# Packed attention and two MLPs on one core: other scratches and step numbers for the weight sums, earlier x loads, another order of the last products

## The chip, the cores and the metric

The kernel runs on one core of a Trainium2 chip. The metric is the time of one execution in device microseconds (us), taken as the median of several runs. Five queues matter: TensorE (PE, with its weight loads as PEld), VectorE (DVE), ScalarE (ACT), GpSimd (POOL, hardly used) and SyncE (SP), which here issues the DMA transfers. Each engine works through its own instructions in the order in which they were written; it waits when the next one needs something that is not there yet, and everything behind that instruction waits too.

## The reference

```python
def sm_attn(qq, kk, vv):
    s = scale * np.matmul(qq, kk.transpose(0, 1, 3, 2))
    s = s - np.max(s, axis=-1, keepdims=True)
    a = np.exp(s)
    a = a / (np.sum(a, axis=-1, keepdims=True) + 1e-09)
    return np.matmul(a, vv)
p_packed = sm_attn(p, k, v)              # p: 32 packed queries a head
x = sm_attn(q, p_packed, p_packed)       # 8 batches, 8 heads, 576 positions, 64 wide
x = heads side by side                   # 4608 x 512
h = x @ w_in                             # first MLP, 512 -> 2048 -> 512, ELU
x = np.where(h > 0, h, np.exp(np.minimum(h, 0)) - 1) @ w_out
h = x @ w_in2                            # second MLP, a rational function of h
P = a[0] + a[1]*h + a[2]*h**2 + a[3]*h**3
Q = 1 + |b[0]|*|h| + |b[1]|*h**2
out = (P / (Q + 1e-6)) @ w_out2
```

The weights come in float64 and everything is computed to float32 accuracy: each float32 operand is split in a high and a low part, and a product is three TensorE products (high by high, high by low, low by high).

## The kernel before

**Two stages.** Stage A (to about 785 us) does the attention and the first MLP. It runs 256 steps, 32 for each of the 8 batches: 16 tiles `f` of the hidden width for each half `n` of a batch's positions. A step is six products into `h` (L391), the ELU on ACT and DVE (L400 to L416), and twelve products into four accumulators `acc` (L426). At the end of each half, `a_evac` copies the accumulators to `x` (L450, L452: two by ACT, two by DVE), and the next step's products into `acc` wait for that. `x_prep` then makes seven combinations of the quarters of `x`, splits each in high and low, and stores them to `x2d` in DRAM (14 transfers of 144 KB, L478). Stage B does the second MLP in 48 pairs of `f` tiles. Its first products go by seven products of sums (P1 to P7, a Strassen scheme) that read the stored `x2d` and weight sums stored in `s2d`; `prod` is at L692, its output products `out_mm` at L767.

**What sets the order.** The program is written by lists of calls keyed to a step: `at(q, s, fn, ...)` puts a call in list `ldq` (loads), `peq` (TensorE) or `ewq` (ACT and DVE) of step `s`. The loop at step `s` runs `ldq`, the `h` products of step `s+2`, `peq`, the splitting of `g` for `s+1`, the ELU for `s+2`, then `ewq`, then the `acc` products of `s`, then `a_evac` if a half ends. Each engine's queue gets its instructions in that order.

**Side work in stage A.** During batches 1 to 4 the loop over `i` makes the sums of the second MLP's input weights. In group `i` four pieces `a21, a22, a11, a12` are loaded into `raw` buffers (`w2_raw`, five steps ahead), turned into float32 by `w2_up` (ACT, L520) and `w2_bits` (DVE, L526, L530), added to `s1..s4` (`w2_sum`, DVE, L629), and each result is split: `w2_hi` (ACT, L634) writes the high part to a tile `whi`, `w2_lo` (DVE, L639) leaves the low part in place and issues two stores of 256 KB on SP (L641). All float32 values live in three scratch tiles `ca`, `cb`, `cc`; a scratch or `whi` is written again only when the store that reads it has landed. In batches 5 to 7 the 16 pieces of the output weights ("o") go the same way to `wo2d`. `load_v`, `load_q1` and, in the last batch, `x_load` (768 KB each, L681, for stage B) share the SP queue with them.

**The end of stage B.** `window(s)` writes pair `s`: P products of pair `s+2`, the function of pair `s+1` on ACT and DVE, and six output products o0 to o5 of pair `s`, in the order of the table `PLAN` (a name ending in 1 or 0 is `f` tile 1 or 0; + is pair `s+2`, - pair `s`, none `s+1`). For `s = 45` the output products are moved: o2 behind P5, o3 to o5 behind all. `tail` writes the last pair's output products, tile 1 first, and the copies and stores of the result, all issued on SP. `WARM` gives the numbers of 128x128 products that are run at the start on a unit matrix; the last entry stands just before the first `h` products.

Of the kernel before, what the change touches and what calls it, by code (L numbers as in the profile page):

```python
# [11 lines left out]
F32R = mybir.dt.float32r  # L12
U32 = mybir.dt.uint32
AF = mybir.ActivationFunctionType
ALU = mybir.AluOpType
# [7 lines left out]
def packed_attention_moe_moe2_kernel(  # L23
# [39 lines left out]
    WARM = (14, 2, 1, 2, 5, 2, 11)  # L63
# [568 lines left out]
    def w2_hi(w):  # L632
        t = T.tile([128, 512], F32R, tag="whi", name=f"whi{w}")
        nc.scalar.copy(t, w2t[w])  # L634
        w2t["hi", w] = t
# [127 lines left out]
    def out_mm(p, i, fs=(1, 0)):  # L763
        for f in fs:
            w = wo2[p, f]
            for k, (g, wx) in enumerate(((0, 0), (0, 1), (1, 0))):
                nc.tensor.matmul(  # L767
                    acc[i], lhsT=g_tile(p, f, g)[:, i * 128:(i + 1) * 128], rhs=w[:, wx, :],
                    start=(p % NPR == 0 and f == 1 and k == 0),
                    stop=(p % NPR == NPR - 1 and f == 0 and k == 2))  # L770
# [3 lines left out]
    def out_ev(p, i, eng, cut=(slice(0, DM),)):  # L774
        o = m2["o"][n_o[0] % 5]
        n_o[0] += 1
        u, end = p // NPR * TU + i % 3 * 128, p // NPR * TU + i % 3 * 128 + 128
        segs = []
        while u < end:
            e = min(end, (u // TR + 1) * TR)  # L780
            segs.append((u, e))
            u = e
        for x in cut:
            (nc.scalar.copy if eng is nc.scalar else nc.vector.tensor_copy)(o[:, x], acc[i][:, x])
            for a, e in segs:
                t0, r = a // TR * TA + i // 3 * TR + a % TR, a - (end - 128)
                nc.sync.dma_start(out=out[t0:t0 + e - a, x], in_=o[r:r + e - a, x])
            eng = nc.vector if eng is nc.scalar else nc.scalar
# [32 lines left out]
    def window(s):  # L821
# [6 lines left out]
        if s == NPAIR - 3:  # L828
            late = [x for x in plan if x[0] in ("o3", "o4", "o5")]
            o2 = plan.index(("o2", s))  # L830
            plan.insert(plan.index(("P5", s + 2)) + 1, ("o2", s))
            del plan[o2]
            plan = [x for x in plan if x not in late] + late
# [6 lines left out]
    def tail():  # L840
        p = NPAIR - 1
        for i in range(6):
            out_mm(p, i, (1,))
        for i in range(6):
            out_mm(p, i, (0,))
            h = DM // 2
            out_ev(p, i, (nc.scalar, nc.vector)[i % 2],
                   (slice(0, h), slice(h, DM)) if i == 5 else (slice(0, DM),))

    with tc.manual_schedule():  # L850
# [193 lines left out]
        for b in range(B - 1):  # L1044
# [18 lines left out]
            if b + 2 < B:  # L1063
                at(ldq, o + (28 if b else 36), load_v, b + 2)
                at(ldq, o + (20 if b else 26), load_k, b + 2)
                at(ldq, o + NS + 10, load_q1, b + 2)
# [8 lines left out]
        def w2_split(s, u, w, dst):  # L1075
            at(ewq, u, w2_hi, w)
            at(ewq, s, w2_lo, w, dst)

        for i in range(4):
# [3 lines left out]
            s1, s2, s3, s4 = (("s", i, j) for j in range(1, 5))  # L1083

# [4 lines left out]
            w2_load(s + 10, a22, "cb")  # L1089
            at(ewq, s + 12, w2_sum, s1, "cc", a21, a22, ALU.add)  # L1090
            w2_split(s + 13, s + 12, a22, dst(P4))
            w2_load(s + 16, a11, "cb")
# [5 lines left out]
            w2_load(s + 32, a12, "cb")  # L1098
            at(ewq, s + 33, w2_sum, s4, "cc", a12, s2, ALU.subtract)
            w2_split(s + 35, s + 34, s2, dst(P6))  # L1100
            w2_split(s + 37, s + 36, a12, dst(P2))
            w2_split(s + 42, s + 41, s4, dst(P3))
        slots = [(5, 11, 12, 13), (5, 16, 18, 19), (5, 23, 25, 29), (5, 31, 32, 33), (6, 6, 7, 8), (6, 10, 11, 12),
                 (6, 13, 14, 16), (6, 23, 25, 29), (6, 31, 32, 33)] + [(7, t, t + 1, t + 2) for t in range(3, 22, 3)]
        for i, (b, s, u, t) in enumerate(slots):
            f = i // 2 + NPR * (i % 2)
            w2_load(b * NS + s, ("o", f), ("ca", "cb", "cc")[i % 3])
            w2_split(b * NS + t, b * NS + u, ("o", f), o2_dst(f))
# [29 lines left out]
        for j in range(5):  # L1138
            at(ldq, o + 2 + 2 * j, x_load, 0, j)
# [114 lines left out]
```

## Time and profile before

| | us |
|---|---|
| median of 3 runs | 1532.81 (1527.85 to 1533.84) |
| the profiled execution | 1534.12 |
| its span, first to last instruction | 1532.2 |
| PE busy | 1477.8 (96%) |
| DVE busy | 1245.3 (81%) |
| ACT busy | 1088.0 (71%) |

The busy shares are means over unlike stages. In stage B a pair takes 15.64 us and TensorE hardly pauses; in stage A it pauses in a few places. What a change is worth is read at those places: which engine waits there, for what, and how much of that TensorE feels.

### The profile page before, as it was taken

The page shows a single profiled execution, that of the slowest core. Times are in us where ns is not written, and L with a number is a line of the kernel's source. Part 1 is how long each engine was busy: PE and PEld are TensorE (multiplying, and loading weights), DVE is VectorE, ACT ScalarE, POOL GpSimd, SP SyncE. Part 2 cuts the span into 40 slices and gives each one's busy share as a digit, 9 for nine tenths or more (in the row PEclk, how much of TensorE's full clock was granted, in tenths as well). Part 3 has the DMA queues.
Part 4 walks back from the last instruction along what each step waited for, and adds up shares of the span by engine and source line. Part 5 has one row for each costly group of instructions (what it writes and reads, how often), then busy time and mean ns, then how long its engine had stood idle before and what let it go on. Part 6 is the DMA issues. An engine that isn't in the chain of part 4 may idle for free.

```text
span 1532.2 us, 26764 instructions
## 1 busy us (share of the span) xinstructions
PE 1477.8 (96%) x10194; PEld 1332.4 (87%) x10194; DVE 1245.3 (81%) x2078; ACT 1088.0 (71%) x1992; POOL 3.3 (0%) x8
## 2 busy tenths in 40 slices
PE   7899999989899899999999999999999999999997
PEld 6778979879798798989989888988899888988896
DVE  6887676866768567776589999999999999999996
ACT  4876666666667567776688787778778777778775
POOL 0000000000000000000000000000000000000000
PEclk8999999999999999999999999999999999999999
DMA  9532554354553454538868866777777686777641
GB/s 346 177 140 70 162 181 137 118 156 144 162 153 115 123 171 153 151 106 281 269 218 278 292 226 223 246 246 240 247 240 250 219 280 211 251 258 229 199 147 46
DMA packets 191264, 301.14 MB, mean 197 GB/s; under 512 B 13472, under 2 KB 131488, under 8 KB 190240
## 3 DMA queue, kind: packets, MB, share of 16 engines
q1 hardware_dynamic: 191136, 299.42, 60.0%
q8 instruction: 81, 1.33, 0.4%
q14 instruction: 47, 0.39, 0.1%
HBM read 233.84 MB, written 65.54 MB: 195 GB/s over the span
## 4 chain that ended last, share of the span: by engine, by line
PE 76%; DMA 8%; DVE 8%; ACT 5%; issue 1%; SPq 1%; ACTq 0%; DVEq 0%
PE bank L692 22%; PE acc L426 18%; PE acc L767 17%; PE h L391 8%; PE acc_h L767 8%; DMA x2d<-x 2%; PE m L347 1%; DVE g L406 1%; DVE gl_all L416 1%; ACT g L401 1%; DVE w L744 1%; PE pp L248 1%; ACT g L400 1%; DMA raw0('o', 0)_112<-in_w_out_dram 1%; ACT gl_all L411 1%
## 5 line engine op out<-in xcount | busy, mean ns | idle before, releaser
L426 PE MATMUL acc<-gl_all,wo 128*128 128x288 f32 x3072 | 462.5, 299 | 31.4 <-ACT x L450 17.6
L426 PEld LDWEIGHTS acc<-gl_all,wo 128*128 128x128 f32 x3072 | 419.0, 190 | 79.6 <-ACT g L401 20.2
L391 PE MATMUL h<-A_flat,m 128*128 128x288 f32 x1536 | 245.6, 295 | 2.2 <-DVE m L361 0.9
L391 PEld LDWEIGHTS h<-A_flat,m 128*128 128x128 f32 x1536 | 217.6, 190 | 4.0 <-DVE m L361 1.7
L767 PE MATMUL acc<-wo,A_flat 128*128 128x512 f32 x768 | 204.2, 393 | 0.0
L692 PE MATMUL bank<-xs_wi,sw 128*128 128x384 f32 x960 | 190.1, 336 | 0.3 <-DVE h L710 0.3
L416 DVE TENSOR_TENSOR gl_all<-g,gl_all 128x288 fp32r<-128x288 f32 x256 | 115.7, 452 | 87.6 <-ACT gl_all L411 87.1
L692 PE MATMUL bank<-xs,sw 128*128 128x384 f32 x912 | 180.0, 336 | 3.7 <-DVE h L710 3.1
L692 PEld LDWEIGHTS bank<-xs_wi,sw 128*128 128x128 f32 x960 | 170.4, 188 | 9.8 <-DVE h L710 0.7
L744 DVE SCALAR_TENSOR_TENSOR w<-w,sq 128x768 f32<-128x768 f32 x192 | 178.8, 952 | 0.0
L406 DVE SCALAR_TENSOR_TENSOR g<-g,h 128x288 f32<-128x288 f32 x256 | 115.8, 452 | 73.2 <-ACT g L401 71.0
L692 PEld LDWEIGHTS bank<-xs,sw 128*128 128x128 f32 x912 | 161.7, 188 | 13.6 <-DVE h L710 4.1
L411 ACT CAST gl_all<-g 128x288 fp32r<-128x288 f32 x256 | 110.7, 433 | 87.4 <-PE acc L426 50.8
L767 PEld LDWEIGHTS acc<-wo,A_flat 128*128 128x128 f32 x768 | 142.5, 188 | 21.4
L400 ACT ACTIVATE g<-h 128x288 f32<-128x288 f32 x256 | 105.1, 410 | 52.0 <-PE h L391 51.5
L401 ACT ACTIVATE g<-g 128x288 f32<-128x288 f32 x256 | 113.9, 445 | 8.1
L767 PE MATMUL acc_h<-wo,A_flat 128*128 128x512 f32 x384 | 104.3, 393 | 0.0
L726 DVE SCALAR_TENSOR_TENSOR w<-sq,cf,w 128x768 f32<-128x768 f32 x96 | 97.5, 1015 | 2.1 <-ACT w L716 0.4
L748 DVE SCALAR_TENSOR_TENSOR t<-t,cf,w 128x768 f32<-128x768 f32 x96 | 97.5, 1016 | 1.7
L740 ACT ACTIVATE sq<-sq,cf 128x768 f32<-128x768 f32 x96 | 89.8, 935 | 1.6
L737 ACT ACTIVATE sq<-w,cf 128x768 f32<-128x768 f32 x96 | 89.8, 935 | 1.1 <-DVE w L726 1.1
L758 ACT CAST A_flat<-t 128x768 fp32r<-128x768 f32 x72 | 60.3, 837 | 36.3 <-DVE t L748 36.3
(419 smaller groups left out, 1957.2 us busy)
## 6 DMA issues: line engine op xcount, KB each, us to landing
sw<-s2d SPq DMA_DIRECT2D x144, 512.0 KB, 4.2
wo<-wo2d SPq DMA_DIRECT2D x96, 512.0 KB, 5.0
x2d<-x SPq DMA_DIRECT2D x210, 144.0 KB, 2.4
xs_wi<-x2d SPq DMA_DIRECT2D x20, 768.0 KB, 7.4
xs<-x2d SPq DMA_DIRECT2D x19, 768.0 KB, 7.4
sw<-s2d SPq DMA_DIRECT2D x48, 256.0 KB, 2.8
q<-in_qT_dram SPq DMA_DIRECT2D x16, 576.0 KB, 5.6
v<-in_v_dram SPq DMA_DIRECT2D x8, 1024.0 KB, 6.5
```

The lines of the kernel that those rows point to most:

```text
L391: nc.tensor.matmul(ps[:, :TA], lhsT=m[:, wx, r, c0:c0 + 128], rhs=A[:, ax, r, :], start=(i == 0), stop=(i == 5))
L400: nc.scalar.activation(d["e"], d["h"][:, :TA], AF.Exp)
L401: nc.scalar.activation(d["e"], d["e"], AF.Relu, scale=-1.0, bias=1.0)
L406: nc.vector.scalar_tensor_tensor(d["g"], d["e"], -1.0, d["h"][:, :TA], ALU.mult, ALU.max)
L411: nc.scalar.copy(d["ghi"], d["g"])
L416: nc.vector.tensor_tensor(d["glo"], d["g"], d["ghi"].bitcast(F32), ALU.subtract)
L426: nc.tensor.matmul(acc[m][:, :TA], lhsT=w[:, wx, m * 128:(m + 1) * 128], rhs=d[g], start=(first and i == 0), stop=(last and i == 2))
L692: nc.tensor.matmul(m2["ab"][bank][:, :TU], lhsT=w[:, j % 2, wx, k, :], rhs=x[:, xx, k, :], start=(start and i == 0), stop=(i == 5), skip_g ...
L726: nc.vector.scalar_tensor_tensor(w, m2["sq", f], cf[:, 5:6], w, ALU.mult, ALU.add)
L744: nc.vector.scalar_tensor_tensor(w, w, c, m2["sq", f], ALU.add, ALU.mult)
L748: nc.vector.scalar_tensor_tensor(t, t, cf[:, 0:1], m2["w", f], ALU.add, ALU.mult)
L767: nc.tensor.matmul(acc[i], lhsT=g_tile(p, f, g)[:, i * 128:(i + 1) * 128], rhs=w[:, wx, :], start=(p % NPR == 0 and f == 1 and k == 0), st ...
```

## The change

It does six things. (1) In the weight sums, scratches `cb` and `cc` take turns: piece a22, a11 and sum s4 go to `ta`, sum s1 and piece a12 to `tb`, and `ta`, `tb` are `cb`, `cc` in even groups and `cc`, `cb` in odd ones. Sum s1 and the split of a22 come a step sooner, the split of s4 too. (2) `load_v` is two steps later in batches 1 to 5. (3) In the last batch the high parts of the o pieces take turns in `whi`, `E` and `aT`. (4) The first five `x_load` calls move from steps 226, 228, 230, 232, 234 to 223, 224, 225, 226, 227. (5) The last `WARM` entry is 8, not 11. (6) At the end, pair 45's o2 to o5 stand among P7, P4 and P3; the window of pair 46 follows a table `LAST` that ends tile 1's function before most of tile 0's; `tail` runs the products with the high part of `g` of several accumulators before those with the low part, and the stores of what ACT copied are issued from ACT's queue.

```diff
-    WARM = (14, 2, 1, 2, 5, 2, 11)
+    LAST = (
+        "C12 Id1 Q1 o0 Ln1 ta1 tb1 o1 Exp1 o2 Sq0 Abs0 Na1 Id0 o3 Nb1 Q0 o4 Ln0 g1 o5 hi1 ta0 Exp0 lo1 tb0 Na0 Nb0 "
+        "g0 hi0 lo0").split()
+    WARM = (14, 2, 1, 2, 5, 2, 8)
...
-    def w2_hi(w):
-        t = T.tile([128, 512], F32R, tag="whi", name=f"whi{w}")
+    def w2_hi(w, tag="whi"):
+        t = T.tile([128, 512], F32R, tag=tag, name=f"whi{w}", bufs=tag_bufs.get(tag, 1))
...
-    def out_mm(p, i, fs=(1, 0)):
+    def out_mm(p, i, fs=(1, 0), ks=(0, 1, 2)):
         for f in fs:
             w = wo2[p, f]
-            for k, (g, wx) in enumerate(((0, 0), (0, 1), (1, 0))):
+            for k in ks:
+                g, wx = ((0, 0), (0, 1), (1, 0))[k]
...
-                nc.sync.dma_start(out=out[t0:t0 + e - a, x], in_=o[r:r + e - a, x])
+                (q and eng is nc.scalar and q or nc.sync).dma_start(
+                    out=out[t0:t0 + e - a, x], in_=o[r:r + e - a, x])
...
         if s == NPAIR - 3:
-            late = [x for x in plan if x[0] in ("o3", "o4", "o5")]
-            o2 = plan.index(("o2", s))
-            plan.insert(plan.index(("P5", s + 2)) + 1, ("o2", s))
-            del plan[o2]
-            plan = [x for x in plan if x not in late] + late
+            for x, y in (("o2", "P7"), ("o3", "P4"), ("o4", "P3"), ("o5", "o4")):
+                plan.remove((x, s))
+                plan.insert(plan.index((y, s + 2 * (y[0] == "P"))) + 1, (x, s))
+        elif s == NPAIR - 2:
+            plan = [(x, s + (x[0] != "o")) for x in LAST]
...
         p = NPAIR - 1
+        for k in (0, 1), (2,):
+            for i in range(6):
+                out_mm(p, i, (1,), k)
+        for k in (0, 1), (2,):
+            for i in range(3):
+                out_mm(p, i, (0,), k)
         for i in range(6):
-            out_mm(p, i, (1,))
-        for i in range(6):
-            out_mm(p, i, (0,))
+            if i > 2:
+                out_mm(p, i, (0,))
...
-                at(ldq, o + (28 if b else 36), load_v, b + 2)
+                at(ldq, o + (30 if b else 36), load_v, b + 2)
...
+            ta, tb = ("cc", "cb") if i % 2 else ("cb", "cc")
...
-            w2_load(s + 10, a22, "cb")
-            at(ewq, s + 12, w2_sum, s1, "cc", a21, a22, ALU.add)
-            w2_split(s + 13, s + 12, a22, dst(P4))
-            w2_load(s + 16, a11, "cb")
+            w2_load(s + 10, a22, ta)
+            at(ewq, s + 11, w2_sum, s1, tb, a21, a22, ALU.add)
+            w2_split(s + 12, s + 11, a22, dst(P4))
+            w2_load(s + 16, a11, ta)
...
-            w2_load(s + 32, a12, "cb")
-            at(ewq, s + 33, w2_sum, s4, "cc", a12, s2, ALU.subtract)
+            w2_load(s + 32, a12, tb)
+            at(ewq, s + 33, w2_sum, s4, ta, a12, s2, ALU.subtract)
...
-            w2_split(s + 42, s + 41, s4, dst(P3))
+            w2_split(s + 41, s + 40, s4, dst(P3))
...
-            w2_split(b * NS + t, b * NS + u, ("o", f), o2_dst(f))
+            w2_split(b * NS + t, b * NS + u, ("o", f), o2_dst(f), ("whi", "E", "aT")[i % 3] if b == B - 1 else "whi")
...
         for j in range(5):
-            at(ldq, o + 2 + 2 * j, x_load, 0, j)
+            at(ldq, o - 1 + j, x_load, 0, j)
```

SP's queue around steps 59 to 66 (the first group; `v` is `load_v`, `s2d` takes a weight sum's two parts, `raw1` is a weight piece), before:

```order
L502 DMA raw1('i', 0, 2)_2637<-in_w_in_dram 128x1024
L478 DMA x2d<-x_47_2259 128x2x144 x4
L128 DMA v_2674<-in_v_dram 128x4x512
L131 DMA v_2674<-in_v_dram 64x512
L641 DMA s2d<-whi('i', 0, 0)_2654 128x4x128
L641 DMA s2d<-w2('i', 0, 0)_cb 128x4x128
L502 DMA raw1('i', 2, 1)_2886<-in_w_in_dram 128x1024
```

and in the change, where the scratch names in the queue show nothing yet, but the two stores stand ahead of `v`:

```order
L505 DMA raw1('i', 0, 2)_2634<-in_w_in_dram 128x1024
L481 DMA x2d<-x_47_2256 128x2x144 x4
L644 DMA s2d<-whi('i', 0, 0)_2651 128x4x128
L644 DMA s2d<-w2('i', 0, 0)_cb 128x4x128
L131 DMA v_2738<-in_v_dram 128x4x512
L134 DMA v_2738<-in_v_dram 64x512
L505 DMA raw1('i', 2, 1)_2883<-in_w_in_dram 128x1024
```

Moved: the stores of piece a11 and `load_v` have changed places; nothing else has at this place.

SP's queue in the last batch, from the load of piece o12 on (`xs_wi` is `x_load`, `wo2d` takes an o piece's two parts, `x2d` the x combinations), before:

```order
L502 DMA raw1('o', 12)_8461<-in_w_out_dram 128x1024
L502 DMA raw1('o', 5)_8564<-in_w_out_dram 128x1024
L641 DMA wo2d<-whi('o', 4)_8547 128x512
L641 DMA wo2d<-w2('o', 4)_cc 128x512
L681 DMA xs_wi<-x2d 128x4x384
L478 DMA x2d<-x_223_8529 128x2x144 x2
L502 DMA raw1('o', 13)_8654<-in_w_out_dram 128x1024
L681 DMA xs_wi<-x2d 128x4x384
L641 DMA wo2d<-whi('o', 12)_8670 128x512
L641 DMA wo2d<-w2('o', 12)_ca 128x512
L478 DMA x2d<-x_223_8529 128x2x144 x4
L681 DMA xs_wi<-x2d 128x4x384
```

and in the change:

```order
L505 DMA raw1('o', 12)_8458<-in_w_out_dram 128x1024
L684 DMA xs_wi<-x2d 128x4x384 x2
L505 DMA raw1('o', 5)_8564<-in_w_out_dram 128x1024
L684 DMA xs_wi<-x2d 128x4x384
L644 DMA wo2d<-whi('o', 4)_8547 128x512
L644 DMA wo2d<-w2('o', 4)_cc 128x512
L684 DMA xs_wi<-x2d 128x4x384
L481 DMA x2d<-x_223_8528 128x2x144 x2
L684 DMA xs_wi<-x2d 128x4x384
L505 DMA raw1('o', 13)_8655<-in_w_out_dram 128x1024
L644 DMA wo2d<-whi('o', 12)_8670 128x512
L644 DMA wo2d<-w2('o', 12)_ca 128x512
```

Moved: four of the x loads now stand ahead of the first `x2d` stores of `x_223`, where one stood.

DVE's queue for the last pair, from the first `ta` that moves (L726 and L729 are `Q`, L730 and L733 `ta`, L734 and L737 `tb`, L744 and L747 `Na` and `Nb`, L748 and L751 `g`, L761 and L764 `lo`; before, `w_9293` and `t_9295` are tile 1 and `w_9296` and `t_9298` tile 0), before:

```order
L730 TENSOR_TENSOR t_9298<-t_9298,h_9666 128x768
L734 SCALAR_TENSOR_TENSOR t_9295<-t_9295,cf,h_9301 128x768
L726 SCALAR_TENSOR_TENSOR w_9296<-sq_9297,cf,w_9296 128x768
L744 SCALAR_TENSOR_TENSOR w_9293<-w_9293,sq_9294 128x768
L734 SCALAR_TENSOR_TENSOR t_9298<-t_9298,cf,h_9666 128x768
L744 SCALAR_TENSOR_TENSOR w_9293<-w_9293,sq_9294 128x768
L744 SCALAR_TENSOR_TENSOR w_9296<-w_9296,sq_9297 128x768
L748 SCALAR_TENSOR_TENSOR t_9295<-t_9295,cf,w_9293 128x768
L744 SCALAR_TENSOR_TENSOR w_9296<-w_9296,sq_9297 128x768
L748 SCALAR_TENSOR_TENSOR t_9298<-t_9298,cf,w_9296 128x768
L761 TENSOR_TENSOR g_9665<-t_9295,A_flat 128x768
L761 TENSOR_TENSOR g_9302<-t_9298,xg_k 128x768
```

and in the change, where `w_9290` and `t_9292` are tile 1, `w_9293` and `t_9295` tile 0:

```order
L733 TENSOR_TENSOR t_9292<-t_9292,h_9298 128x768
L737 SCALAR_TENSOR_TENSOR t_9292<-t_9292,cf,h_9298 128x768
L747 SCALAR_TENSOR_TENSOR w_9290<-w_9290,sq_9291 128x768 x2
L729 SCALAR_TENSOR_TENSOR w_9293<-sq_9294,cf,w_9293 128x768
L751 SCALAR_TENSOR_TENSOR t_9292<-t_9292,cf,w_9290 128x768
L733 TENSOR_TENSOR t_9295<-t_9295,h_9663 128x768
L764 TENSOR_TENSOR g_9662<-t_9292,A_flat 128x768
L737 SCALAR_TENSOR_TENSOR t_9295<-t_9295,cf,h_9663 128x768
L747 SCALAR_TENSOR_TENSOR w_9293<-w_9293,sq_9294 128x768 x2
L751 SCALAR_TENSOR_TENSOR t_9295<-t_9295,cf,w_9293 128x768
L764 TENSOR_TENSOR g_9299<-t_9295,xg_k 128x768
```

Moved: tile 1's `lo`, which was next to last, now has only one `Q` and one `ta` of tile 0 ahead of it.

## Rows read from the trace of the kernel before

**Rows 1.** The page's first part: busy time, share, instructions of each engine.

```profile
PE 1477.8 (96%) x10194; PEld 1332.4 (87%) x10194; DVE 1245.3 (81%) x2078; ACT 1088.0 (71%) x1992; POOL 3.3 (0%) x8
```

**Rows 2.** Waits: engine, line, waited for; us in total, times, longest.

```profile
PE acc L426 <- ACT x L450: 17.6, 4, 5.0
...
ACT w2('i', 1, 3)_cb L520 <- DMA s2d<-w2('i', 1, 1)_cb: 5.4, 1, 5.4
...
ACT whi('o', 6)_8956 L634 <- DMA wo2d<-whi('o', 13)_8870: 4.7, 1, 4.7
...
ACT whi('i', 2, 3)_3299 L634 <- DMA s2d<-whi('s', 0, 4)_3198: 3.9, 1, 3.9
```

**Rows 3.** SP's timeline at 221 us: start, duration, what was issued.

```profile
221.30 0.37 SPq L128 DMA_DIRECT2D v<-in_v_dram  x1
```

**Rows 4.** The chain that ended last, same place: start, duration, what.

```profile
222.97 6.58 DMA s2d<-w2('i', 0, 0)_cb
```

**Rows 5.** PE's timeline: first and fourth such place, a step with `s1h`, undisturbed steps.

```profile
224.44 1.72 PE L426 MATMUL acc<-gl_all,wo 128*128 128x288 f32 x12
...
235.18 1.01 PE L426 MATMUL acc<-gl_all,wo 128*128 128x288 f32 x5
...
505.59 1.72 PE L426 MATMUL acc<-gl_all,wo 128*128 128x288 f32 x12
...
513.11 3.25 PE L426 MATMUL acc<-gl_all,wo 128*128 128x288 f32 x12 [5.02 <-ACT x L450]
...
518.81 0.40 PE L426 MATMUL acc<-gl_all,wo 128*128 128x288 f32 x1
...
328.55 0.72 PE L182 MATMUL s1h<-k,p 64*32 64x288 f32 x16
...
687.18 1.72 PE L426 MATMUL acc<-gl_all,wo 128*128 128x288 f32 x12
...
691.91 1.72 PE L426 MATMUL acc<-gl_all,wo 128*128 128x288 f32 x12
```

**Rows 6.** Busy time by stretch (PE, PEld, DVE, ACT, POOL), granted clock, DMA share, GB/s.

```profile
515.50:517.00 1.50, 1.50 (x8) 1.50 (x8) 1.47 (x4) 0.43 (x1) 0.00 (x0) 0.50 0.31 98
```

**Rows 7.** PE's timeline at 271 us, where ACT's wait for `whi` of a22 ends.

```profile
271.06 0.40 PE L426 MATMUL acc<-gl_all,wo 128*128 128x288 f32 x1 [0.52 <-ACT gl_all L411]
```

**Rows 8.** PE's timeline in the last batch, steps 235, 239 and 244.

```profile
715.31 1.72 PE L426 MATMUL acc<-gl_all,wo 128*128 128x288 f32 x12
...
727.70 2.19 PE L426 MATMUL acc<-gl_all,wo 128*128 128x288 f32 x12 [2.37 <-ACT gl_all L411]
...
740.96 1.74 PE L426 MATMUL acc<-gl_all,wo 128*128 128x288 f32 x12
```

**Rows 9.** DMA issues of 684 to 712 us: count, KB each, us to landing.

```profile
xs_wi<-x2d SPq DMA_DIRECT2D x4, 768.0 KB, 5.9
...
wo2d<-whi('o', 5)_8766 SPq DMA_DIRECT2D x1, 256.0 KB, 8.2
```

**Rows 10.** SP's timeline in the last batch: the first x load.

```profile
694.54 0.39 SPq L681 DMA_DIRECT2D xs_wi<-x2d  x1
```

**Rows 11.** PE's timeline at the start: the last `WARM` products.

```profile
23.20 4.60 PE L914 MATMUL warm<-ident 128*128 128x128 f32 x22
```

**Rows 12.** DVE's timeline at the start.

```profile
24.05 0.76 DVE L338 TENSOR_TENSOR A_flat<-s2y,A_flat 128x576 fp32r<-128x576 f32 x1 [0.16 <-ACT A_flat L333]
...
29.54 0.45 DVE L406 SCALAR_TENSOR_TENSOR g<-g,h 128x288 f32<-128x288 f32 x1 [1.02 <-ACT g L401]
```

**Rows 13.** PE's timeline at the end: P3, pair 46's output products, pair 47's.

```profile
1503.42 1.31 PE L692 MATMUL bank<-xs,sw 128*128 128x384 f32 x6 [1.69 <-DVE h L710]
...
1511.41 5.60 PE L767 MATMUL acc<-wo,A_flat 128*128 128x512 f32 x24
...
1517.94 0.50 PE L767 MATMUL acc_h<-wo,g 128*128 128x512 f32 x1 [0.48 <-DVE g L761]
```

**Rows 14.** SP's timeline at the end: the last two stores.

```profile
1527.47 1.22 SPq L787 DMA_DIRECT2D out_dram<-h_o  x2
```

More of the change, by code (lines that the diff above doesn't have):

```diff
@@ L772, in packed_attention_moe_moe2_kernel, with out_ev @@
     n_o = [0]
-    def out_ev(p, i, eng, cut=(slice(0, DM),)):
+    def out_ev(p, i, eng, cut=(slice(0, DM),), q=None):
         o = m2["o"][n_o[0] % 5]
@@ L841, in tail @@
         p = NPAIR - 1
+        for k in (0, 1), (2,):
[4 more added lines that the diff above has]
+                out_mm(p, i, (0,), k)
         for i in range(6):
-            out_mm(p, i, (1,))
-        for i in range(6):
-            out_mm(p, i, (0,))
+            if i > 2:
+                out_mm(p, i, (0,))
             h = DM // 2
             out_ev(p, i, (nc.scalar, nc.vector)[i % 2],
-                   (slice(0, h), slice(h, DM)) if i == 5 else (slice(0, DM),))
+                   (slice(0, h), slice(h, DM)) if i == 5 else (slice(0, DM),),
+                   nc.scalar)
     with tc.manual_schedule():
@@ L1073, in w2_load, with w2_split @@
             at(ewq, s, w2_bits, piece)
-        def w2_split(s, u, w, dst):
-            at(ewq, u, w2_hi, w)
+        def w2_split(s, u, w, dst, tag="whi"):
+            at(ewq, u, w2_hi, w, tag)
             at(ewq, s, w2_lo, w, dst)
```

## The prediction

> **What bounds the kernel now.** I read the page's busy shares first: TensorE is busy for 96% of the span [rows 1], so nothing short of its own pauses is worth much, and the question is where these are. The list of waits answers it: one entry, the `acc` products waiting for ACT's copies of the accumulators (L450), holds 17.6 us in four waits [rows 2]. The same list says what ACT waits for just before: `w2_up` of piece a12 into `cb`, held by the landing of the store of `cb`'s old content (a11). There are four such rows, one for each group, of 4.0, 4.8, 5.0 and 5.4 us; the longest is shown [rows 2]. SP's timeline and the chain show why that store is late: the 1 MB load of `v` is issued 1.67 us ahead of it and the store lands 6.58 us after issue [rows 3, 4]. So the order is: `v` load, store, `w2_up`, `a_evac`, `acc`. Shorter ACT waits of the same sort stand for `whi`, in the groups (3.9 us) and in the last batch (4.7 us) [rows 2].
>
> **Part (1) and (2), the four long waits.** I take the price from TensorE's clock time, not from its idle time, since it restarts slowly. Two undisturbed steps take 691.91 - 687.18 = 4.73 us, and `s1h`, which stands in this stretch, about 0.64 (0.72 less the 0.08 by which neighbours overlap): 5.37 [rows 5]. The first place took 235.18 - 224.44 = 10.74, the fourth 518.81 - 505.59 = 13.22 [rows 5]: 5.4 and 7.85 lost, the least and the most by ACT's waits, mean 6.6, so 26.4 for four. That is more than 17.6 because the clock granted right after such a pause was 0.50, 1.2 GHz instead of 2.4 [rows 6]. In the change a12 goes to `tb`, whose last store (of s1) was issued six steps before, some 14 us, and the a11 store goes ahead of `v`. `w2_up` then has nothing to wait for, and ACT reaches the copies before the accumulators are done. What takes the store's place: s4 now overwrites a11's scratch, four steps (9.4 us) after a11's store, on DVE; with `v` behind it, the store should be down by then. `v` itself is used 11 steps later. At 687 to 692, where a half ends with nothing late, TensorE loses nothing [rows 5]. I take 26, bounds 20 (one of four places finds another late transfer) and 27.
>
> **Part (1), the two-step reuse.** ACT's 3.9 us wait for `whi` (four rows, 3.5 to 3.9) is the s4 store standing behind the load of `q`. TensorE felt 0.52 of it [rows 2, 7]. In the change s4's split comes a step sooner, ahead of `q`, and DVE's sum s1 stands two steps behind that store as before; were it to wait, the low parts of `g` queued behind it on DVE, and so `acc`, would wait too. Four places of 0.5 or a little more: 1.8, bounds 0 (s1 waits again) and 2.7. `q` and the a11 load behind it come a good microsecond later; their users stand about four steps on, so I cost that at nothing; if the cover is gone, ACT waits, and up to 2 us of that is free, as the next part shows.
>
> **Parts (3) and (4), the last batch.** From step 235 at 715.31 to step 244 at 740.96 there are nine steps in 25.65 us [rows 8]; nine undisturbed ones take 9 x 2.365 = 21.3 by rows 5. So 4.4 are lost, nearly all in two `whi` waits and their wake; the longer, 4.7 us on ACT, left TensorE idle for 2.37 [rows 2, 8], so some 2.3 us of an ACT wait cost nothing. With three tiles in turn, a high part is overwritten nine steps after the last, over 20 us: those waits go, +4.4. Against it stands the x loads' move. Before, the first one is issued at 694.54, right ahead of the first x stores of that half [rows 10]; in the change four are ahead of these stores, the first two some ten microseconds before them. A transfer of 256 KB behind two x loads took 8.2 us to land, an x load itself 5.9 [rows 9], so each x load that is still in the queue adds about 3. One more than before will be: the x stores land up to 3 us later, twice an ACT step of `x_prep` waits for them, and 3 - 2.3 = 0.7 is felt each time: -1.4. Later, in exchange, the queue is emptier. Sum +3.0, bounds +4.4 and -4 (four ACT steps that each wait a whole x load, 5.9 - 2.3 = 3.6, less the gain).
>
> Here a rule of the Trainium skill speaks against the change. The rows show transfers landing in the order of issue, the store after the x loads ahead of it [rows 9]. "DMA: Bandwidth & Descriptors", section "Queues, rings and completion order", says that on each DMA engine descriptors are consumed in ring order, though completion is not first in, first out. Taken strictly, the x stores pay for every x load moved ahead of them, and this part would give the lower bound, -4, and a total near 1506; if they passed the loads, it would give +4.4 and a total near 1498. The rows lie between, as the early loads have had time to drain.
>
> **Part (5), the start.** The last `WARM` row is 22 passes in 4.60 us, 0.209 each; three products are six passes, 1.25 us [rows 11]. What they cover: the last input of the first `h` is ready at 24.05 + 0.76 = 24.8, while the row runs to 27.8 [rows 11, 12]. So `h` starts 1.25 earlier. The next consumer is DVE, which idled 1.02 before it [rows 12]; the rest is its own queue. I take 0.8, bounds 0 and 1.25.
>
> **Part (6), the end.** P3 starts 1.69 us late, held by DVE [rows 13]. DVE's order up to there is unchanged, so P3 stays where it is; the gain is that o3 now runs in front of it. Six of the 24 products that take 5.60 us are 1.4 us [rows 13]. Then pair 47's low part of tile 1 no longer comes last but one in the function: by DVE's queue four operations of some 0.95 us fewer stand ahead of it, so the 0.48 pause and its restart, 0.7 together, go [rows 13]. Tile 0's parts come some 0.8 us later than before, but TensorE needs them only after tile 1's 18 products. The last two stores take 1.22 us of SP's queue, one behind the other [rows 14]; on two queues the last is issued up to 0.6 sooner, but ACT's copies now stand behind ACT's issues, which may cost as much: +0.1. No ACT issue is in the trace; its nearest row is SP's 0.61 each. Sum 2.2, bounds 1 and 3.
>
> **Sum.** 26 + 1.8 + 3.0 + 0.8 + 2.2 = 33.8. The profiled execution took 1534.12 with a span of 1532.2; 1534.1 - 33.8 = 1500.3. The median of the runs is 1.3 lower than that execution, so the forecast is 1499.
>
> **Rivals.** (a) The queue gives it back: x loads, `q` and `v` moved in front of or behind other transfers make new ACT waits in the last batch and in the groups. Price: part (4) at -4 instead of +3, the short waits at 0, one long place kept: 7 + 2 + 6 = 15, so 1503 to 1514. For it speaks that an ACT wait stops `a_hi` and `a_evac` alike; against it that 2.3 us of each are free. (b) The long waits stay, because what held ACT was not the scratch but the piece's own load, or the sum's wait moves to DVE: only parts (4) to (6) and half of the rest would come, some 12 us: 1515 to 1526. Against it: the list of waits names the store, and with it the same scratch, in all four. (c) Slower than before: without its pauses TensorE is granted less clock. Place: the rest of the program, stage B above all; price: each microsecond of its work done at 1.2 GHz costs one more, so from 34 us of such work on the gain is gone, 1533 and more. Against it: the clock in the rows fell after pauses, not after work [rows 6], and stage B runs without pauses now.
>
> **How the numbers follow.** The forecast has 0.80, (a) 0.14, (b) 0.04, (c) 0.02. A range of 1493 to 1508 holds the forecast with its bounds (all lows of the parts do not meet; about 9 above, 6 below with the run-to-run spread of before, 1527.85 to 1533.84) and the half of (a) below 1508. Half a per cent, 7.7 us, is about what a measurement of this kernel can tell from no change. All of the forecast and of (a), and (b) below 1525, are faster: 0.97. The same: 0.02. Slower: 0.01.
>
> **What would show it.** In the profile after: no wait of `acc` for L450 over 1 us, and no ACT wait of `w2_up` for an `s2d` store; the stretch that now runs from 505.59 to 518.81 shorter by over 6 us; ACT waiting for x stores in the last batch no more than about 3 us each; TensorE's last pause before P3 shorter by 1.4, and none for tile 1's low part. I am wrong if `acc` waits for L450 again behind another transfer, if waits for `x2d` stores in the last batch add up to more than 10 us, or if the granted clock falls in stage B.

## The result, and the profile after

The changed kernel takes 1496.18 us (median of 4 runs, 1495.55 to 1496.71), the kernel before 1532.87 in the same session: ratio 0.9767, 95% interval 0.9745 to 0.9788. The forecast was 1499 with a range of 1493 to 1508. Below, "after" is the changed kernel; its line numbers are higher than those of before: by 3 in stage A, by 3 to 5 in stage B, by 11 for the warm passes (L914 is L925).

The page's busy times of after, against [rows 1]: the same work in a span of 1493.8 instead of 1532.2.

```profile
PE 1465.7 (98%) x10188; PEld 1325.1 (89%) x10188; DVE 1246.8 (83%) x2078; ACT 1087.0 (73%) x1992; POOL 3.3 (0%) x8
```

The list of waits of after (engine, line, waited for; us in total, times, longest), against [rows 2]:

```profile
ACT x L476 <- DMA x2d<-x: 18.2, 10, 2.9
...
PE acc L429 <- ACT gl_all L414: 2.6, 4, 1.1
...
DVE h_o L788 <- DMA out_dram<-h_o: 2.3, 1, 2.3
...
ACT whi('o', 3)_7946 L637 <- DMA wo2d<-whi('o', 10)_7848: 1.6, 1, 1.6
...
PE acc L429 <- ACT x L453: 0.4, 1, 0.4
```

Of the 17.6 us in which `acc` waited for ACT's copies, 0.4 is left. The `whi` waits of 3.9 and 4.7 are gone. ACT still waits for x stores: over the whole span 18.2 in ten waits, where it was 15.1, none longer than 2.9.

TensorE's timeline of after at the first and the fourth long place (start, duration, what), against [rows 5]:

```profile
222.86 1.72 PE L429 MATMUL acc<-gl_all,wo 128*128 128x288 f32 x12
...
228.27 1.83 PE L429 MATMUL acc<-gl_all,wo 128*128 128x288 f32 x12
...
482.02 1.72 PE L429 MATMUL acc<-gl_all,wo 128*128 128x288 f32 x12
...
487.44 1.83 PE L429 MATMUL acc<-gl_all,wo 128*128 128x288 f32 x12
```

These take 5.41 and 5.42 us, where they took 10.74 and 13.22; the working from undisturbed steps had given 5.37.

TensorE's timeline of after at the end, against [rows 13]:

```profile
1467.35 1.31 PE L695 MATMUL bank<-xs,sw 128*128 128x384 f32 x6 [1.14 <-DVE h L713]
...
1473.98 5.60 PE L771 MATMUL acc<-wo,A_flat 128*128 128x512 f32 x24
1479.42 1.07 PE L771 MATMUL acc_h<-wo,A_flat 128*128 128x512 f32 x4
```

From P3 to the 24 products is 6.63 us, where it was 7.99: 1.36 less. The pause for tile 1's low part, 0.48, is gone. The pause before P3 is 0.55 shorter (1.14 for 1.69), since o2 now stands behind P7 and takes the place of another pause of before, in front of P4:

```profile
1500.42 1.32 PE L692 MATMUL bank<-xs,sw 128*128 128x384 f32 x6 [0.57 <-ACT s L707]
```

P3 starts 8.25 behind P6, where it was 8.26: it stays in its place, and the gain is that o3 now runs ahead of it.

**One table for all kernels.** Rows that each trace has cut the span into five stretches that add up to it: to the second row of `s1h`; on to the last row of `m` products (the groups, where the four long places lie); on to the first P product of stage B (the last batch); on to the end of the last product (stage B); and the rest (the last stores). The last column is the median time of all executions; the five stretches are those of the profiled one. The last batch of after, for one, is 716.82 - 651.41 = 65.41.

| kernel | start | groups | last batch | stage B | stores | time |
|---|---|---|---|---|---|---|
| before | 61.33 | 622.38 | 69.15 | 773.13 | 6.21 | 1532.87 |
| after | 59.73 | 591.68 | 65.41 | 770.92 | 6.06 | 1496.18 |
| after_again | 59.90 | 592.13 | 64.53 | 770.95 | 6.29 | 1495.06 |
| e_scratch | 60.23 | 595.58 | 68.90 | 773.74 | 5.45 | 1505.37 |
| e_v | 59.83 | 595.29 | 70.62 | 773.11 | 5.45 | 1505.56 |
| e_steps | 59.59 | 615.93 | 68.92 | 773.14 | 6.32 | 1526.90 |
| u_xload | 59.76 | 592.50 | 64.64 | 770.96 | 6.74 | 1496.52 |
| u_whi | 59.98 | 592.04 | 64.73 | 770.94 | 6.01 | 1496.21 |
| u_both | 60.37 | 591.80 | 69.53 | 770.99 | 6.11 | 1500.60 |
| u_warm | 60.25 | 590.76 | 64.35 | 770.96 | 6.28 | 1494.37 |
| u_tail | 59.94 | 591.70 | 64.26 | 773.07 | 6.13 | 1497.71 |
| best | 60.32 | 592.07 | 68.20 | 770.97 | 6.74 | 1498.50 |
| lo_first | 60.51 | 592.32 | 64.24 | 770.99 | 6.24 | 1496.95 |
| lo_first_22 | 60.51 | 590.72 | 65.85 | 770.93 | 6.29 | 1495.63 |

Between the first two rows the groups gave 30.7, the last batch 3.7, the start 1.6, stage B 2.2, the stores 0.15: 38.4 of span.

### The profile page after: what moved, and what is told of

It is laid out like the page before. It is cut to its first block, busy times and chain, and to the rows that moved or that the text cites. A ratio compares the mean times of both kernels' runs of the same rounds, so it can differ in the third digit from the quotient of the medians.

```text
span 1493.8 us, 26767 instructions
## 1 busy us (share of the span) xinstructions
PE 1465.7 (98%) x10188; PEld 1325.1 (89%) x10188; DVE 1246.8 (83%) x2078; ACT 1087.0 (73%) x1992; POOL 3.3 (0%) x8
## 4 chain that ended last, share of the span: by engine, by line
PE 87%; DVE 6%; ACT 4%; DMA 2%; issue 1%; ACTq 0%; POOL 0%; DVEq 0%; POOLq 0%
PE acc L429 23%; PE bank L695 23%; PE acc L771 17%; PE h L394 11%; PE acc_h L771 9%; PE m L350 2%; DMA x2d<-xpart 1%; PE pp L251 1%; DVE g L409 1%; DMA x2d<-x 1%; PE s L285 1%; DMA s2d<-w2('i', 2, 2)_cb 1%; DVE gl_all L419 0%; DVE w L747 0%; PE warm L925 0%
## 5 line engine op out<-in xcount | busy, mean ns | idle before, releaser
L429 PE MATMUL acc<-gl_all,wo 128*128 128x288 f32 x3072 | 455.9, 297 | 8.3 <-DVE gl_all L419 2.9
L747 DVE SCALAR_TENSOR_TENSOR w<-w,sq 128x768 f32<-128x768 f32 x192 | 178.9, 952 | 0.1
L419 DVE TENSOR_TENSOR gl_all<-g,gl_all 128x288 fp32r<-128x288 f32 x256 | 115.8, 452 | 60.4 <-ACT gl_all L414 59.7
L751 DVE SCALAR_TENSOR_TENSOR t<-t,cf,w 128x768 f32<-128x768 f32 x96 | 97.5, 1016 | 1.7
L729 DVE SCALAR_TENSOR_TENSOR w<-sq,cf,w 128x768 f32<-128x768 f32 x96 | 97.4, 1015 | 1.6
L761 ACT CAST A_flat<-t 128x768 fp32r<-128x768 f32 x72 | 60.3, 838 | 35.0 <-DVE t L751 35.0
```

Source lines behind the costliest of these rows:

```text
L419: nc.vector.tensor_tensor(d["glo"], d["g"], d["ghi"].bitcast(F32), ALU.subtract)
L429: nc.tensor.matmul(acc[m][:, :TA], lhsT=w[:, wx, m * 128:(m + 1) * 128], rhs=d[g], start=(first and i == 0), stop=(last and i == 2))
L729: nc.vector.scalar_tensor_tensor(w, m2["sq", f], cf[:, 5:6], w, ALU.mult, ALU.add)
L747: nc.vector.scalar_tensor_tensor(w, w, c, m2["sq", f], ALU.add, ALU.mult)
L751: nc.vector.scalar_tensor_tensor(t, t, cf[:, 0:1], m2["w", f], ALU.add, ALU.mult)
```

## The experiments

**Which half removes the long waits?** The change does two things about them, and the prediction credited both together. Each was tried alone on the kernel before. e_scratch:

```diff
+            ta, tb = ("cc", "cb") if i % 2 else ("cb", "cc")
-            w2_load(s + 32, a12, "cb")
-            at(ewq, s + 33, w2_sum, s4, "cc", a12, s2, ALU.subtract)
+            w2_load(s + 32, a12, tb)
+            at(ewq, s + 33, w2_sum, s4, ta, a12, s2, ALU.subtract)
```

(cut: a22 and a11 go to `ta`, s1 to `tb`; no step is moved)

> The kernel before with the turn of the two scratch tiles alone (a12 goes to the tile of s1, s4 to the tile of a11); the load of v stays ahead of the a11 store, and every step stays. Theory A (the wait sits in the choice of scratch): w2_up of a12 finds its tile free, the store of a11, 6.6 us under way, is down before DVE writes s4 over it 9.4 us later; all four long places go, -26, about 1507, no wait of acc for L450. Theory B (it sits in the queue): the store behind v is still late, and now DVE waits for it with the s4 sum; part of the 17.6 us of waits comes back under DVE's name, -10 or less, 1523 or more.

e_v:

```diff
-                at(ldq, o + (28 if b else 36), load_v, b + 2)
+                at(ldq, o + (30 if b else 36), load_v, b + 2)
```

> The kernel before with the load of v two steps later alone, behind the a11 store; scratches and steps as before. Theory A (scratch): w2_up of a12 comes two steps (4.7 us) after the store's issue and is still close behind it; some waits of 1 to 2 us stay, acc feels part: -15 to -20, 1513 to 1518. Theory B (queue): without the 1 MB ahead of it the store lands in some 2 to 3 us like others of its size, before w2_up comes; all four long places go with this one number, -24 to -26, 1507 to 1509. That both the turn and the place of v do it alone would mean that the gains of the two do not add.

Measured: 1505.37 (ratio 0.9817, 0.9803 to 0.9832) and 1505.56 (0.9819, 0.9805 to 0.9834). Either one does the whole of it, and e_scratch's second theory, that DVE would wait in ACT's place, falls; the four places give 26.3 us in both traces. They do not add. Why, the store of a11's low part tells. SP's timeline of e_scratch (start, duration, what):

```profile
220.12 0.37 SPq L128 DMA_DIRECT2D v<-in_v_dram  x1
...
221.78 0.44 SPq L641 DMA_DIRECT2D s2d<-w2('i', 0, 0)_cb  x1
```

and of e_v:

```profile
219.65 0.36 SPq L641 DMA_DIRECT2D s2d<-w2('i', 0, 0)_cb  x1
220.23 0.75 SPq L128 DMA_DIRECT2D v<-in_v_dram  x1
```

The same store in the list of DMA issues (KB each, us to landing), of e_scratch:

```profile
s2d<-w2('i', 0, 0)_cb SPq DMA_DIRECT2D x1, 256.0 KB, 6.3
```

and of e_v:

```profile
s2d<-w2('i', 0, 0)_cb SPq DMA_DIRECT2D x1, 256.0 KB, 2.4
```

In e_scratch the store is as late as in before (6.3 behind `v`; [rows 4] has 6.58), but nobody needs its tile. In e_v the tile is needed as soon as before, but the store lands in 2.4, at 222.05, and `w2_up` comes at 223.66. e_v's first theory, that waits of 1 to 2 us would stay, falls.

**The two-step reuse.** e_steps:

```diff
-            at(ewq, s + 12, w2_sum, s1, "cc", a21, a22, ALU.add)
-            w2_split(s + 13, s + 12, a22, dst(P4))
+            at(ewq, s + 11, w2_sum, s1, "cc", a21, a22, ALU.add)
+            w2_split(s + 12, s + 11, a22, dst(P4))
...
-            w2_split(s + 42, s + 41, s4, dst(P3))
+            w2_split(s + 41, s + 40, s4, dst(P3))
```

> The kernel before with the sum s1, the split of a22 and the split of s4 one step sooner, nothing else. The prediction gave these places 1.8 in all (0 to 2.7); between the two traces TensorE gained 4.4 there. If the step alone does it, -4.4, about 1528.5, with gains of 0.8 to 1.6 at each of the four places and the ACT waits for whi gone. If the prediction's size was right and the rest came from the scratches, -2 or less, 1531 or more.

Measured: 1526.90, ratio 0.9957 (0.9942 to 0.9972), 6.1 us less; at the four places alone 1.59, 1.11, 1.34 and 1.34, together 5.4. The size in the prediction was wrong. Rows of before that it had not used show the rest. From the list of waits:

```profile
DVE w2('s', 1, 1)_cc L629 <- DMA s2d<-w2('s', 0, 4)_cc: 4.2, 1, 4.2
DVE w2('s', 2, 1)_cc L629 <- DMA s2d<-w2('s', 1, 4)_cc: 3.8, 1, 3.8
DVE w2('s', 3, 1)_cc L629 <- DMA s2d<-w2('s', 2, 4)_cc: 3.7, 1, 3.7
```

and from TensorE's timeline, the row after that of [rows 7]:

```profile
271.92 1.70 PE L426 MATMUL acc<-gl_all,wo 128*128 128x288 f32 x11 [0.47 <-DVE gl_all L416]
```

At three of the four places DVE waited for the same s4 store as ACT, and TensorE for DVE, behind its wait for ACT. With the split a step sooner all of these rows are gone from e_steps' list, and ACT's `whi` waits too. The fourth place has no such wait of DVE, since no s1 follows, and still gave 1.34. There TensorE shows one pause of 0.34, and two rows of twelve products take longer than the 1.72 to 1.74 of the rows between:

```profile
554.41 2.21 PE L426 MATMUL acc<-gl_all,wo 128*128 128x288 f32 x12 [0.34 <-ACT gl_all L411]
...
559.64 2.19 PE L426 MATMUL acc<-gl_all,wo 128*128 128x288 f32 x12
```

So DVE's wait is a part of what was missing, not the whole: the listed pause is not the whole price even where ACT alone was late.

**The last batch: again two edits for one wait.** u_xload and u_whi undo one each in the changed kernel, u_both undoes both:

```diff
-            at(ldq, o - 1 + j, x_load, 0, j)
+            at(ldq, o + 2 + 2 * j, x_load, 0, j)
```

```diff
-            w2_split(b * NS + t, b * NS + u, ("o", f), o2_dst(f), ("whi", "E", "aT")[i % 3] if b == B - 1 else "whi")
+            w2_split(b * NS + t, b * NS + u, ("o", f), o2_dst(f))
```

> The changed kernel with the five loads of x of the last batch back in their old places (two steps apart, three steps later). Read between the traces, the sooner loads cost TensorE 0.6 us around the first x stores and the whi tiles gained 4.4. If that reading is right: -0.6, about 1495.6, the x2d wait of 1.7 us on ACT near the first store gone and no new ones. If the order of the queue decides more than that (each x load in front of a store costs a whole transfer), undoing gives -3 or more. If the sooner loads are what keeps later stores and stage B's first loads on time, undoing costs: +1 to +3, with longer x2d waits later in the batch.

> The changed kernel with one whi tile in the last batch, as before, instead of three in turn. Theory A (the three tiles brought what the last batch gained, and the x loads' move has little to do with it): the two ACT waits for wo2d stores are back, some 3.4 and 4.7 us, TensorE loses 4.4 at the same two places: about 1500.6. Theory B (the sooner x loads make these stores later too, so that the tiles pay for them as well): longer waits, more than two of them, 6 to 8 lost: 1502 to 1504.

> The changed kernel with both edits of the last batch undone, the whi tiles and the x loads. Theory A (either one alone removes the waits): the stretch from the last m product row to the first P product of stage B takes 69 to 70.6 as in before and in the three kernels made from it (69.2, 68.9, 70.6, 68.9), the two waits for wo2d stores are back, about 1500. Theory B (neither matters; the waits went because the batch starts in another place against the transfers): 64.3 to 65.5, 1496.

Measured: 1496.52, 1496.21 and 1500.60 (ratios 0.9764, 0.9771 and 0.9801). Undoing one costs nothing that can be told, undoing both brings the batch from 64.5 and 65.4 back to 69.5. In u_both ACT's two waits for `whi` are back:

```profile
ACT whi('o', 13)_8867 L637 <- DMA wo2d<-whi('o', 5)_8763: 4.0, 1, 4.0
...
ACT whi('o', 6)_8953 L637 <- DMA wo2d<-whi('o', 13)_8867: 3.5, 1, 3.5
```

In u_whi one of 0.3 is all that is left:

```profile
ACT whi('o', 6)_8953 L637 <- DMA wo2d<-whi('o', 13)_8867: 0.3, 1, 0.3
```

So u_whi's two theories fall both: with one tile and the loads sooner there are no long `whi` waits. SP's timeline shows how, in u_both:

```profile
675.39 0.48 SPq L684 DMA_DIRECT2D xs_wi<-x2d  x1
675.98 0.49 SPq L505 DMA_DIRECT2D raw1('o', 6)_8748<-in_w_out_dram  x1
676.52 0.42 SPq L684 DMA_DIRECT2D xs_wi<-x2d  x1
677.04 0.80 SPq L644 DMA_DIRECT2D wo2d<-whi('o', 5)_8763  x1
```

and in u_whi:

```profile
676.53 0.40 SPq L505 DMA_DIRECT2D raw1('o', 6)_8750<-in_w_out_dram  x1
677.25 0.33 SPq L644 DMA_DIRECT2D wo2d<-whi('o', 5)_8765  x1
```

The DMA issues (count, KB each, median us to landing) of u_both: piece o5's store, then the fourteen x stores of that half in their three bursts, the first two, the next four and the last eight:

```profile
wo2d<-whi('o', 5)_8763 SPq DMA_DIRECT2D x1, 256.0 KB, 9.4
...
x2d<-x SPq DMA_DIRECT2D x2, 144.0 KB, 5.6
...
x2d<-x SPq DMA_DIRECT2D x4, 144.0 KB, 3.0
...
x2d<-x SPq DMA_DIRECT2D x8, 144.0 KB, 6.6
```

and the same of u_whi:

```profile
wo2d<-whi('o', 5)_8765 SPq DMA_DIRECT2D x1, 256.0 KB, 4.2
...
x2d<-x SPq DMA_DIRECT2D x2, 144.0 KB, 7.1
...
x2d<-x SPq DMA_DIRECT2D x4, 144.0 KB, 2.1
...
x2d<-x SPq DMA_DIRECT2D x8, 144.0 KB, 3.5
```

In the old places two x loads of 768 KB go out within 1.2 us, with one weight load between them, right ahead of piece o5's store: 9.4 us to its landing, and ACT waited 4.0 for the tile. Moved sooner, they are down by then: the last of them landed at 673.27 in u_whi, and the store took 4.2. The x stores split. The first two, which now stand behind more loads, take 7.1 instead of 5.6; the twelve behind them land sooner. What the first two cost can be read in after: ACT waits 1.66 for one of them, and TensorE's steps at 671.32 and 674.01 take 2.69 and 2.51, where both take 2.34 in u_xload. That is 0.5.

Are the old places dearer with three tiles, too? best has the x loads of u_xload and, up to stage B, the same code; its batch took 68.2 against 64.6. Its row in the list of waits:

```profile
ACT x L476 <- DMA x2d<-x: 17.4, 10, 4.4
```

and in TensorE's timeline:

```profile
709.97 3.40 PE L429 MATMUL acc<-gl_all,wo 128*128 128x288 f32 x12 [2.37 <-ACT gl_all L414]
```

Here ACT waited 4.4 for one x store and TensorE 2.37 for ACT; in after a wait of 2.45 at this place cost 0.32. So some 2.1 us of an ACT wait are free at this place, about as the prediction had it (2.3); at the first x stores 1.66 cost 0.5, so that figure doesn't hold everywhere. The DMA issues show what came late: the first load of `xs` for stage B, right ahead of that store, in best and then in u_xload:

```profile
xs<-x2d SPq DMA_DIRECT2D x1, 768.0 KB, 7.4
```

```profile
xs<-x2d SPq DMA_DIRECT2D x1, 768.0 KB, 5.3
```

What was issued ahead of it had landed by 703.41 in best, by 703.83 in u_xload, so that no x load from an old place was still in its way. The six traces with the loads sooner and three tiles lie between 64.2 and 65.9; but best's profiled execution was the slowest of its four (1496.84 to 1500.13), and lo_first, with the loads sooner, has one of 1500.23 that was not profiled. That the old places made best's batch longer is not shown.

**The end.** u_tail has the window order and `tail` of the kernel before.

> The changed kernel with the end of the kernel before: o3 to o5 at the end of the third last window, the plan of the last pair as in every other window, products by tile, all stores on the queue of SP. The two traces give 1.36 for o3 in front of P3, 0.82 for tile 1 first, about 0.15 for the stores: 2.3, about 1498.5, the pauses of 1.69 before P3 and 0.48 before the low part of tile 1 back. If P3 stays early, DVE's order in the windows before it had moved as well: +1 or less.

Measured: 1497.71 (ratio 0.9780, 0.9765 to 0.9794). The times differ by 1.5 and 2.7 from the two of after; the table is sharper: stage B takes 773.07 and, in every trace with the new end, 770.92 to 770.99. The new end is worth 2.1 to 2.2; its parts were not tried one by one.

best also copies the last output tile to a free tile, by DVE alone, since in after DVE's last copy waited 2.32 us for the last store from its buffer:

```diff
-        o = m2["o"][n_o[0] % 5]
+        o = m2["w", 0][:, :DM] if p == NPAIR - 1 and i == 5 else m2["o"][n_o[0] % 5]
...
-            eng = nc.vector if eng is nc.scalar else nc.scalar
```

> The changed kernel with the x loads in their old places, and at the very end the last output tile copied by DVE alone in two halves to a tile that is free (w of f tile 0) instead of an output buffer whose last store is still under way; both halves stored by SP's queue. In the trace of the changed kernel DVE's last copy waits 2.32 us for that store and the last copy, on ACT, waits for DVE. Expected: the last copy ends at about 1.6 us sooner, and the span is 1.3 shorter by this and 0.8 shorter by the x loads, together about 1494.2. If the last store's landing is held by the stores ahead of it, 0.5 or less from the end.

Measured: 1498.50 (ratio 0.9785, 0.9769 to 0.9801); beside the batch's loss, the stores took 6.74 from the last product, not less (u_xload, without this edit: 6.74). The last copy does end sooner (0.8 after the last product's end, against 2.5 in after), but the transfers don't. The last 9 us of after, then of best, in 40 slices (busy tenths of the DMA engines, and GB/s):

```profile
DMA  0000000019899898978999998988999830000000
GB/s 0 0 0 0 0 0 0 0 55 264 228 282 301 237 291 291 346 237 246 282 337 310 291 328 282 328 282 310 351 346 319 287 132 27 5 0 0 0 0 0
```

```profile
DMA  0000019899899986799998989999733210000000
GB/s 0 0 0 0 0 55 273 228 291 282 228 310 319 310 228 191 246 291 346 309 364 264 264 264 278 319 319 346 260 109 123 100 50 23 5 0 0 0 0 0
```

From the first output store on, the DMA engines are mostly busy to 80 or 90% for some 5 us: the 1.57 MB of output, more than the copy that comes last, set the end. The thin tail in best's row, where the engines are busy to 30% and less, is not explained. Two queues show no gain over one: 6.0 to 6.7 with two, 5.45 to 6.3 with SP's alone; but the kernels with SP's alone also have the old order of the last products.

**The start.** u_warm has 22 warm passes again (`WARM` ending in 11). lo_first moves the first step's high and low part ahead of the second softmax on DVE; lo_first_22 is that with 22 passes; after_again is the changed kernel once more, beside them.

> The changed kernel with 22 warm passes in the last row instead of 16. Theory A, the prediction's: six passes at 0.209 delay the first h by 1.25 and the end by about 0.8: 1497.0. Theory B: the row's price is not fixed. In the five traces with the 22 passes so far (before and four others are not all alike: 4.60, 3.83, 3.38, 2.72 us) the first h started between 24.2 and 27.6, as the clock rose sooner or later, and DVE held the second acc product in all but one at 32.1 to 32.7; then 22 passes cost the end 0 to 0.4: 1496.2 to 1496.6.

> The changed kernel itself once more, on the chip and beside the runs of before that the next three are compared with. From the first ACT step of the last batch to the first product of the last x_prep's end (the stretch from the last m product row to the first P product of stage B) it took 65.4 us in the first trace; the kernels with one of the two edits of that batch undone took 64.6, 64.7 and, with the same x loads as the 64.6, 68.2. Expected: 1495 to 1497, and 64.3 to 65.5 for the stretch if the sooner loads make it steady; 68 if it is as unsteady with them.

```diff
-            if 0 <= s + 1 < NA:
+            if 0 < s + 1 < NA:
...
                 a_dve1(s + 2)
+            if s == -2:
+                a_hi(0)
+                a_lo(0)
             run(ewq, s)
```

> The changed kernel with the high and the low part of the first g put one step sooner into ACT's and DVE's order, ahead of the second softmax's chain on DVE. In all traces so far the second acc product of the first step waits 1.96 us for that low part, which stands behind this chain, and begins at 32.1 to 32.8. If DVE holds the start there: the product at about 30.4, and up to 1.8 sooner by 60 us into the run, less 0.45 by which the chain is later: about -1.3, 1494.9. If the work behind it (the second half's h, which needs the chain) holds the start: 0 to -0.4.

> As the kernel before this one, with 22 warm passes instead of 16. If the passes delay the start once DVE no longer holds it: +0.7 to +1.25 against 16 passes. If the clock that the passes bring up pays that back: within 0.4 of it. The kernel with 22 passes alone was at 1494.37, below the changed kernel; if that was no effect of the passes, this one comes out at or above the one with 16.

Measured: u_warm 1494.37 (1493.57 to 1494.92; ratio 0.9758), after_again 1495.06 (0.9763), lo_first 1496.95 (0.9778), lo_first_22 1495.63 (0.9765). The warm row and the first `h` in e_steps (22 passes), u_warm (22) and after (16), against [rows 11]:

```profile
21.76 2.72 PE L914 MATMUL warm<-ident 128*128 128x128 f32 x22
24.24 1.05 PE L391 MATMUL h<-A_flat,m 128*128 128x288 f32 x6
```

```profile
22.20 3.74 PE L925 MATMUL warm<-ident 128*128 128x128 f32 x22
25.70 1.04 PE L394 MATMUL h<-A_flat,m 128*128 128x288 f32 x6
```

```profile
22.09 2.54 PE L925 MATMUL warm<-ident 128*128 128x128 f32 x16
24.38 1.03 PE L394 MATMUL h<-A_flat,m 128*128 128x288 f32 x6
```

The same 22 passes take 2.7 to 4.6 us, by the clock granted meanwhile: 1.00 of 2.4 GHz over this row in e_steps, 0.71 in u_warm, 0.57 in before. The Trainium skill, "TensorE: Matmul & The Clock Gate", section "What's actually happening", says that the cold stretch is a matter of time, not of a number of matmuls, and varies from run to run. The six rows with 22 passes, 2.72 to 4.60 us, agree that it varies; the first half of the sentence no run here tests. By 60 us the four kernels with 22 passes and the old order on DVE other than before are at 59.6 to 60.25, the seven with 16 at 59.7 to 60.4: no gain of the edit can be told. lo_first shows why an earlier product does not help either: its first twelve `acc` products run from 30.84, where eleven of them waited until 32.20 in after, and TensorE then waits 1.03 and 1.70 for DVE; by 60 us it is 0.6 to 0.8 behind after and after_again. So that one place in DVE's order does not hold the start; that DVE's work as a whole does is likely, but not shown.

What is not explained: the two kernels of the changed form with 22 passes spend 590.7 and 590.8 in the groups, the eight with 16 passes 591.7 to 592.5. The largest part lies near 180 us, long after the warm row, where ACT's `w2_up` of piece (0, 0) waits 0.8 to 1.6 for a weight store with 16 passes and 0.3 with 22. In before and the three kernels made from it, all with 22, that wait is 0.25 to 0.71, so that the six traces with 22 passes and the eight with 16 do not overlap in it. No run here tells why. In time, too, the 22 passes come out ahead, if anything: u_warm is 0.7 and 1.8 below the two medians of the changed kernel and lies wholly below u_whi, which ran beside it (1493.57 to 1494.92 against 1495.48 to 1497.64); lo_first_22 is 1.3 below lo_first. The cut to 16 passes may thus have cost a microsecond rather than gained one; the intervals against before overlap, so this is not settled.

## Why the prediction was right, and where its steps were off

The sum was 33.8, made on the profiled execution of before. The measured difference is 36.7 by the medians and 38.4 by the spans of the two traces. Point by point:

- **The four long waits: right.** 26 predicted, 26.3 in the trace, and the priced mechanism (pause plus restart) held place by place. What the prediction did not see is that its two reasons, the other scratch and the place of `v`, are two cures of one wait; each alone gives all.
- **The two-step reuse: mis-sized.** 1.8 with a bound of 2.7; it measured 4.4 in after and 5.4 alone. The step that failed is "four places of 0.5 or a little more" and, for s1, "were it to wait": it took TensorE's first idle row as the price, and treated as a possibility a DVE wait of about 4 us that the list of waits already held, at three of the four places. The fourth, without that wait, gave 1.34 as well, so that the idle row alone was too low a price there, too.
- **The last batch: the direction was right, the balance wrong.** +3.0 predicted, 3.7 between the two first traces, and 4.7 between the mean of the five traces with the old batch (69.4) and of the eight with at least one edit, best left aside (64.75; with best 65.1, so 4.3). Between the two first traces the places of the two `whi` waits gave the 4.4 that was predicted for the tiles. But the x loads were priced as a loss alone, -1.4. "One more than before will be" was right for the first two x stores, 1.5 us later and not 3, which cost 0.5. The step that failed is "later, in exchange, the queue is emptier", which the sum put at nothing: the twelve x stores behind them and piece o5's store land sooner, and by u_whi the loads' move alone removes both `whi` waits but for 0.3. So the two edits are again two cures of one wait. Landing in the order of issue, which the prediction took from the trace beside the Trainium skill's rule ("DMA: Bandwidth & Descriptors", section "Queues, rings and completion order"), still holds for every transfer of SP's from 652 to 716 us in u_both and u_whi. But the total near 1506 that a strict reading would give did not come: the loads moved sooner had landed (673.27 in u_whi) when piece o5's store went out (677.25), and could no longer delay it.
- **The start: not shown.** 0.8 predicted; 1.6 lay between the two traces, but the kernels that differ from before elsewhere only reached that point 1.1 to 1.7 sooner too. The price of 0.209 a pass was that of the longest warm row of all. u_warm and lo_first_22 point the other way, if any.
- **The end: right.** 2.2 predicted; 2.2 between the two traces in stage B and 2.1 by u_tail. P3 stayed in its place, as it said; only its sign, a pause before P3 shorter by 1.4, was wrong (0.55, and the 0.57 before P4). Of its +0.1 for the second queue nothing is to be seen.
- **The rivals.** None came. (a) was wrong in its core: the only cost of a moved transfer that was found is the 0.5 of the x loads. ACT's waits for x stores in the last batch of after are 1.66, 2.45 and 2.87, together 7.0, where the prediction would have called itself wrong from 10 on. Against (b), no `w2_up` wait for a store over 0.8 is left in after, and e_scratch and e_v each remove all four long waits. Against (c), the mean granted clock went from 0.989 to 0.996, and in stage B it is 1.00 in both.

By the two traces the sum is 4.6 short: reuse 2.6, start 0.8, last batch 0.7, the long waits and the end the rest. The time lies only 2.8 below the forecast because the trace of before was 1.3 above its median, which the forecast took off, while the trace of after is 0.6 below its own. That the miss looks so small is in part luck.

## What to carry to other kernels

A wait for a buffer has two cures, a longer way to the reuse and a shorter way for the transfer that frees it; price them as one gain, not two, and keep the one that costs less. When a late transfer is found, read the whole list of waits for its name: every engine that waits for it belongs to the price. Price what a moved transfer frees as well as what it delays. And compare a first stretch over several traces before pricing it from one.

## What the runs showed of the hardware

- Transfers that SP issues land in the order of issue, in every row from 652 to 716 us of u_both and u_whi. A store of 256 KB took 9.4 us to land behind two loads of 768 KB and one of 512 KB, and 4.2 where the two of 768 KB were down already.
- One issue does not always take SP the same time. Of the eight x stores behind the crowded loads in u_both, the first five took 0.62 to 0.76 us each and the last three 0.36; in u_whi seven took 0.39 to 0.45 and one 0.96. Why is not shown.
- The same 22 warm passes take 2.72 to 4.60 us by the clock that is granted when they run, and the first `h` behind them starts between 24.2 and 27.6.
- At the very end 1.57 MB of output leave at about 300 GB/s, and with neither a second issuing queue nor a last copy that ends 1.7 us sooner did the last landing come sooner.
